# Mamba2 scan and gated feed-forward on one core: two pieces for weight blocks 8 to 11, a split join, and another order in the first scan

## The chip, the cores and the metric

The kernel runs on one core of a Trainium2 chip. The metric is the device time of one execution in microseconds (us); lower is better. Engines are TensorE (PE; its weight loads are listed as PEld), VectorE (DVE), ScalarE (ACT), GpSimd (POOL) and SyncE (SP), which here only issues transfers. SPq and DVEq stand for the sequencers of these engines. PSUM is the memory that PE writes its results to.

## The reference

```python
def _attn_ref(x, a, B, C):              # batch 4, 8 heads, 768 steps, 32 wide, state 16
    log_a = np.log(np.clip(a, 1e-06, 1.0))
    for c in range(nc):                 # chunks of 32 steps
        ...
        cum = np.cumsum(la, axis=-1)
        L = np.exp(cum[:, :, :, None] - cum[:, :, None, :]) * causal
        CB = np.einsum('bhin,bhjn->bhij', Cc, Bc)
        y_intra = np.einsum('bhij,bhjd->bhid', CB * L, xc)
        y_inter = np.einsum('bhin,bhnd->bhid', Cc, state) * decay_to_i[:, :, :, None]
        ...
        state = decay_full[:, :, None, None] * state + np.sum(Bx, axis=2)

def _moe_ref(x, w_in, w_out):           # 3072 tokens, 256 -> 2048 -> 256
    h = x @ w_in
    g = h * (1.0 / (1.0 + np.exp(-1.702 * h)))
    return (g @ w_out).astype(np.float32)
```

The scan's output (batch, step, head, width) is read as 3072 tokens of 256 values, the `x` of the second part. w_in and w_out come as float64.

## The kernel before, in words

**Groups.** The 3072 tokens are treated in six groups of 512 (`TG`). A group is made of two pairs, a pair being two chunks of 128 steps of one batch. For a group the kernel runs the scan of its two pairs, then the feed-forward. In the first group, `hidden(0, f)` makes `h` for one block of 128 hidden units after another, f = 0 to 15 (L878), each followed by the Silu on ACT, and `project_all(0, ...)` multiplies by w_out, again f = 0 to 15 (L976, tile `o`). Later groups use a form with seven products of sums of blocks (`X`, `Y`, `acc`), which needs all weights.

**Order.** Every engine executes its instructions in the order in which the program writes them (`in_order`). Where a piece of work stands in the text therefore decides what it can hold up. Work that goes with the first group's matmuls is put between blocks by `at(in_hidden[0], f, ...)`, which means after block f of `h`, and `at(in_project[0], f, ...)`, which means before block f of `o`.

**Weights.** The float64 weights are fetched as pairs of 32-bit words (`bits`) and made float32 on the chip. `PIECES` lists the pieces: of w_in blocks 0-1, 2-3, 4-5 and 6-7 (two blocks each), then 8-11 and 12-15 (four each); of w_out four pieces of four. `fetch(i)` issues two transfers on SP's queue. Then:

- `fields(i)`, VectorE, L193 and L196: exponent and mantissa bits out of the high words (tiles `p`, `m`);
- `clamp(i)`, ACT, L204 and L205: two steps on the exponent;
- `rounded(i)`, VectorE, L209: the low word is added to the mantissa;
- `join(i, parts)`, VectorE, L223 and L229: sign, exponent and mantissa become the weights, in one or several parts, two instructions for each part.

`narrow(i)` is the step of the schedule: it rounds piece i, joins it, and takes the fields of piece i + 1. For some pieces the join stands ahead of the next piece's fields, for others behind. In the kernel before the pieces that join first are 2, 4, 5 and 6; for piece 3 (blocks 6 and 7) the fields of piece 4 (blocks 8 to 11) come first. The pieces share four buffers, and a pair of two-block pieces shares one; `NEXT` says which piece is fetched after which join. Between piece 6 and its fields, `decay_rows(0)` runs for the next scan.

**First scan.** The first group's scan (pairs 0 and 1) is written out by hand at L1154 and below. Its steps: decays `L` from masked differences on PE and an exponential on ACT (L557); B and C transposed on VectorE (L597); `CT`, C masked by chunk part, for pair 0 (`mask_first(0)`) and pair 1 (`mask_first(1)`), both on POOL (L632); `pick_a`, copies of a picked by chunk part for the next group's decays (two ACT instructions, L364, tile `X`); `clip(az1)`, VectorE L354, which goes before it; `turn_back`, B back through PE (L609); `score`, the products of C and B (L664, tile `cb`, one area for both pairs); `since_first`, the running decay (`rows`, L515, and its exponential L520); `gain`, the chunks' states (L695, tile `A`, from x and `Be`); `weigh`, L times cb on VectorE (L675); `parts_first` and `since_start`, L649 on POOL, tile `CsT`; a scan over chunk states (L717) and `keep_first` with the states `S`; and in `finish`, `intra` (L818), `inter` (L804) and the copy of the result to `yT` (L838), with `fan_all` (L418) between the two pairs' `intra`. `dense(8, ...)` (L1150) is a product of ones into a PSUM bank that nobody reads. `fold_ident(1)` (L336) makes the second half of a constant that the next group's scan uses.

**x.** `load(p, "x")` issues two transfers of 128 KB for each pair, on SP.

Of the kernel before, what the change touches and what calls it, by code (L numbers as in the profile page):

```python
# [8 lines left out]
FP32 = mybir.dt.float32  # L9
# [26 lines left out]
def kernel(  # L36
# [101 lines left out]

    def load(p, parts=None):
        if parts is None:  # L140
            parts = "bcx" if p < 2 * PG else "bx"
            if p >= 2 * PG:
                load_blocks(p)
        for part in parts:
            dst, src, e = {"b": (rb, B, N), "c": (rc, C, N), "x": (rx, x, D)}[part]
            dst[p] = raw.tile([P, 2, NH, e], FP32, tag=part, name=f"{part}{p}",
                              bufs=2 if part == "c" else 3)
            for k in range(2):
                b, c = divmod(2 * p + k, NC)
                sl = slice(c * P, (c + 1) * P)  # L150
                nc.sync.dma_start(out=dst[p][:, k], in_=src[b, :, sl, :].rearrange("h s d -> s h d"))


    assert NF == 4 * CG
    PIECES = [("in", f, 2) for f in range(0, 8, 2)] + [("in", 8, 4), ("in", 12, 4)] \
        + [("out", f, 4) for f in range(0, NF, 4)]
# [56 lines left out]

    NEXT = {1: (6,), 5: (9,)}

    def join(i, parts=1):

        name, f, n = PIECES[i]
        n //= parts
        low, m, p2 = bits.pop(i)[1], mantissa.pop(i), power.pop(i)  # L220
        for k in range(parts):
            cols, fs = slice(k * n * DM, (k + 1) * n * DM), slice(f + k * n, f + (k + 1) * n)
            nc.vector.scalar_tensor_tensor(out=p2[:, cols], in0=low[:, cols], scalar=0x80000000,  # L223
                                           in1=p2[:, cols], op0=ALU.bitwise_and, op1=ALU.bitwise_or)
# [4 lines left out]
            nc.vector.scalar_tensor_tensor(  # L229
                out=dst, in0=m[:, cols].bitcast(FP32).rearrange("p (h e) -> p h e", h=h),  # L230
                scalar=2.0 ** -20, in1=p2[:, cols].bitcast(FP32).rearrange("p (h e) -> p h e", h=h),
                op0=ALU.mult, op1=ALU.mult)
        for n in NEXT.get(i, ()):
            fetch(n)

    def narrow(i):
        rounded(i)
        if i in (2, 4, 5, 6):
            join(i, 2 if i in (4, 5) else 1)
        if i == 6:  # L240
            decay_rows(0)
        if i + 1 < len(PIECES):
            fields(i + 1)
        if i not in (2, 4, 5, 6):
            join(i, 2 if i == 3 else 1)

# [37 lines left out]
    def table(f):  # L284

        nc.scalar.activation(early, early, f)
# [5 lines left out]
    load(0, "x")  # L292
    load(1, "x")

# [39 lines left out]
    def fold_ident(k, engine=nc.vector):  # L334
# [9 lines left out]
    nc.scalar.activation(cum, az0, AF.Ln)  # L344
    table(AF.Exp)
    nc.vector.tensor_tensor_scan(
        out=cum.rearrange("p k s -> p (k s)"), data0=carry.rearrange("p k s -> p (k s)"),
# [3 lines left out]

    def clip(t):

        nc.vector.tensor_scalar(out=t, in0=t, scalar1=1e-6, scalar2=1.0,  # L354
                                op0=ALU.max, op1=ALU.min)
        nc.vector.memset(t.rearrange(by_chunk, s=2)[:, :, :, 0], 0.0)

    def pick_a(p):

        assert divmod(2 * p, NC) == (0, CG)  # L360
        X = ffn.tile([P, 2, DM], FP32, tag="ob", name=f"X{p}")
        X = fans[p] = X.rearrange("p k (q i) -> p k q i", q=Q)
        for q in range(Q):
            nc.scalar.activation(X[:, :, q], az1, AF.Copy, scale=pick1[:, q:q + 1])  # L364

# [57 lines left out]
    def fan_all(p):  # L423

        ab = area(f"ab{p}")[:, :, :2 * Q * H]
        for r in range(R):
            fan(p, r, ab[:, r])
        fans[p] = ab

    def decay_fanned(p):  # L430
# [78 lines left out]
    def since_first():  # L509

        since[0] = ssd.tile([P, NC, P], FP32, tag="since", name="since0")
        rows = [bank(f"rows{p}")[:, :2 * P] for p in range(PG)]
        for p in range(PG):
            at = slice(32 * p, 32 * p + 32)
            nc.tensor.matmul(out=rows[p],  # L515
                             lhsT=whose[at, p].rearrange("p h n -> p (h n)"),
                             rhs=cum[at].rearrange("p k s -> p (k s)"), start=True, stop=True,
                             tile_position=(32 * p, 0), skip_group_check=True)
        for p in range(PG):
            nc.scalar.activation(since[0][:, 2 * p:2 * p + 2].rearrange("p c s -> p (c s)"),  # L520
                                 rows[p], AF.Exp)

    def drops():
# [102 lines left out]
    def mask_first(p):  # L626

        s = st[p]
        s["CT"] = ssd.tile([P, 2, Q, P], FP32, tag="CT", name=f"CT{p}")
        if p:  # L630
            nc.vector.memset(s["CT"][:, 0, 0, :1], 0.0)
        nc.gpsimd.tensor_tensor(  # L632
            out=s["CT"], in0=s["tp"].unsqueeze(2).to_broadcast([P, 2, Q, P]),
            in1=part.unsqueeze(1).unsqueeze(3).to_broadcast([P, 2, Q, P]), op=ALU.mult)
# [15 lines left out]

    def score(pairs, between=lambda: None, to=None):

        cb = (to or area(f"cb{pairs[0]}")).rearrange("p r (k e) -> p r k e", k=2 * PG)
        for n, p in enumerate(pairs):
            s = st[p]
            BT, CT = s["BT"], s.pop("CT")
            s["cb"] = cb[:, :, 2 * n:2 * n + 2]
            if n:
                between()
            for k in range(2):  # L660
                for i, side in enumerate(SIDES):
                    for r in range(R):
                        rows = slice(32 * r, 32 * r + 32)
                        nc.tensor.matmul(  # L664
                            out=s["cb"][side, r, k].rearrange("p (q i) -> p q i", q=Q),
                            lhsT=BT[rows, k, side], rhs=CT[rows, k, :, side],
                            start=True, stop=True, tile_position=(32 * r, H * i),
                            skip_group_check=True)
# [13 lines left out]

    def gain(pairs, to=None):
# [3 lines left out]
        for n, p in enumerate(pairs):  # L687
            Be = BE.pop(p)[0]
            for k in range(2):
# [80 lines left out]
    def finish(pairs, steps=range(2)):  # L770
# [39 lines left out]
        def intra(n, p):  # L810
            L = Ls[p]
            for k in range(2):
                for h in range(NH):
                    for i, side in enumerate(SIDES):
# [13 lines left out]
        if early:  # L828
            for n, p in enumerate(pairs):
                if n:  # L830
                    fan_all(PG)
                intra(n, p)
            for n, p in enumerate(pairs):
                for i in range(2):
                    inter(n, p, (i,))
            for t in range(NK):
                for i in range(2):
# [323 lines left out]
    turn_first("B")  # L1161
    clip(az1)
    differ_of(0)
# [5 lines left out]
    fields(0)  # L1169
    mask_first(1)  # L1170
    pick_a(PG)
# [41 lines left out]
    def store_a():  # L1213
# [14 lines left out]
    pairs = PG, PG + 1  # L1228
    at(in_project[0], 0, lambda: turn(PG), lambda: rounded(8),
       lambda: join(8), lambda: fields(9))  # L1230
    at(in_project[0], 1, lambda: clamp(9))
# [3 lines left out]
    at(in_project[0], 5, lambda: narrow(9))  # L1235
    at(in_project[0], 10, lambda: score(pairs), lambda: gain(pairs), lambda: keep_both(pairs, True),
# [203 lines left out]
```

## Time and profile before

| | before |
|---|---|
| runs, us | 346.44, 349.93, 346.78 |
| median, us | 346.78 |
| profiled execution, us | 347.67 |
| its span, first to last instruction, us | 345.9 |
| PE busy, share of the span | 98% |
| VectorE, ACT, POOL busy | 74%, 45%, 5% |
| granted clock | 1.00 |
| first `h` matmul of group 0, us from the start | 17.89 |
| first `o` matmul of group 0 | 47.23 |

Timeline rows read: start, length in us, engine, line, operation, tile written and tiles read, shape and count, and in brackets the idle time before it with what ended it. Rows of one line are put together where they follow each other, so a row's length with "x24" is that of 24 instructions. In the list of waits each line has the total in us, the number of waits and the longest. In the table of stretches each engine has its busy time and, in brackets, its instructions, followed by the granted clock, the mean share of the 16 DMA engines and the rate in GB/s.

### The profile page before, as it was taken

The page shows a single profiled execution, that of the slowest core. Times are in us where ns is not written, and L with a number is a line of the kernel's source. Part 1 is how long each engine was busy: PE and PEld are TensorE (multiplying, and loading weights), DVE is VectorE, ACT ScalarE, POOL GpSimd, SP SyncE. Part 2 cuts the span into 40 slices and gives each one's busy share as a digit, 9 for nine tenths or more (in the row PEclk, how much of TensorE's full clock was granted, in tenths as well). Part 3 has the DMA queues.
Part 4 walks back from the last instruction along what each step waited for, and adds up shares of the span by engine and source line. Part 5 has one row for each costly group of instructions (what it writes and reads, how often), then busy time and mean ns, then how long its engine had stood idle before and what let it go on. Part 6 is the DMA issues. An engine that isn't in the chain of part 4 may idle for free.

```text
span 345.9 us, 8116 instructions
## 1 busy us (share of the span) xinstructions
PE 339.2 (98%) x3380; PEld 270.2 (78%) x3380; DVE 256.1 (74%) x484; ACT 155.1 (45%) x352; POOL 16.7 (5%) x40
## 2 busy tenths in 40 slices
PE   8999999999999999999999999999999999999996
PEld 6633744555788888888888888888888888899996
DVE  5988999999799998858995667787564654465463
ACT  5786771507454324754332554442454322554320
POOL 7300110300000100000000000000000000000000
PEclk9999999999999999999999999999999999999999
DMA  6698899545637100435603036400000300000401
GB/s 160 132 289 211 217 239 133 152 67 102 122 63 127 36 0 15 65 99 100 110 27 51 2 78 121 64 0 3 0 4 2 62 2 0 0 2 0 63 0 62
DMA packets 90004, 25.76 MB, mean 74 GB/s; under 512 B 73416, under 2 KB 87248, under 8 KB 89968
## 3 DMA queue, kind: packets, MB, share of 16 engines
q1 hardware_dynamic: 89104, 24.72, 35.0%
q10 hardware_dynamic: 832, 0.52, 0.5%
q8 instruction: 26, 0.43, 0.5%
q14 instruction: 10, 0.08, 0.1%
q0 software_dynamic: 32, 0.01, 0.0%
HBM read 22.00 MB, written 3.24 MB: 73 GB/s over the span
## 4 chain that ended last, share of the span: by engine, by line
PE 92%; DMA 3%; SPq 2%; DVE 1%; issue 0%; ACT 0%; POOL 0%; DVEq 0%
PE acc L1039 28%; PE X L934 19%; PE Y L944 14%; PE o L976 8%; PE acc L1046 7%; PE h L878 7%; DMA bits<-in_moe_w_in_dram 3%; PE y L818 2%; PE cb L664 2%; SPq L181 1%; PE y L804 1%; PE A L695 1%; PE ab L536 1%; DMA az<-in_a_dram 1%; POOL CsT L649 0%
## 5 line engine op out<-in xcount | busy, mean ns | idle before, releaser
L939 ACT ACTIVATE ac<-X 128x256 f32<-128x256 f32 x76 | 29.1, 383 | 81.7 <-PE X L934 81.0
L1039 PE MATMUL acc<-mg,mw 128*128 128x256 f32 x192 | 54.5, 379 | 0.0
L1066 DVE TENSOR_TENSOR gT<-Y,ac 128x512 f32<-128x512 f32 x38 | 26.2, 689 | 38.1 <-PE Y L944 32.5
L911 ACT ACTIVATE gT<-gT 128x512 f32<-128x512 f32 (+1 forms) x76 | 38.9, 519 | 29.3 <-DVE gT L1066 28.8
L934 PE MATMUL X<-my,mi 128*128 128x256 f32 x152 | 45.2, 380 | 0.0
L1039 PEld LDWEIGHTS acc<-mg,mw 128*128 128x128 f32 x192 | 36.6, 190 | 4.9
L1066 DVE TENSOR_TENSOR gT<-Y,b 128x256 f32<-128x256 f32 x38 | 15.8, 419 | 28.5 <-PE Y L944 28.5
L878 PE MATMUL h<-yT,w_in 128*128 128x512 f32 (+1 forms) x92 | 35.5, 541 | 1.4 <-DVE w_in L229 0.9
L1039 PE MATMUL acc<-gT,w_out 128*128 128x256 f32 x128 | 35.5, 380 | 0.0
L878 PEld LDWEIGHTS h<-yT,w_in 128*128 128x128 f32 x92 | 17.2, 190 | 18.2 <-issue 12.8
L934 PEld LDWEIGHTS X<-my,mi 128*128 128x128 f32 x152 | 28.0, 190 | 4.0 <-ACT ac L939 0.3
L976 PE MATMUL o<-gT,w_out 128*128 128x512 f32 x64 | 28.3, 596 | 0.0
L902 DVE TENSOR_TENSOR mg<-gT 128x512 f32<-128x512 f32 x40 | 27.2, 681 | 0.0
L1039 PEld LDWEIGHTS acc<-gT,w_out 128*128 128x128 f32 x128 | 24.3, 190 | 3.4 <-ACT yT L853 0.2
L939 ACT ACTIVATE b<-X 128x256 f32<-128x256 f32 x38 | 14.6, 383 | 20.8 <-PE X L934 20.3
L934 PE MATMUL X<-yT,w_in 128*128 128x256 f32 x76 | 23.2, 389 | 0.0
L944 PE MATMUL Y<-yT,w_in 128*128 128x256 f32 x76 | 22.7, 381 | 0.0
L944 PE MATMUL Y<-my,mi 128*128 128x256 f32 x76 | 22.7, 381 | 0.0
L934 PE MATMUL X<-my,w_in 128*128 128x256 f32 x76 | 22.5, 380 | 0.0
L944 PE MATMUL Y<-yT,mi 128*128 128x256 f32 x76 | 22.5, 380 | 0.0
L976 PEld LDWEIGHTS o<-gT,w_out 128*128 128x128 f32 x64 | 11.9, 190 | 13.6 <-issue 12.7
L408 DVE TENSOR_TENSOR_SCAN L<-a,idents 128x1024 f32<-128x1024 f32 x9 | 20.5, 2279 | 0.3 <-DMA a<-scratch 0.3
(152 smaller groups left out, 547.8 us busy)
## 6 DMA issues: line engine op xcount, KB each, us to landing
a<-scratch SPq DMA_DIRECT2D x18, 256.0 KB, 4.9
bits<-in_moe_w_out_dram SPq DMA_DIRECT2D x8, 512.0 KB, 7.4
x<-in_x_dram SPq DMA_DIRECT2D x24, 128.0 KB, 3.7
out_dram<-ob SPq DMA_DIRECT2D x40, 64.0 KB, 2.0
bits<-in_moe_w_in_dram SPq DMA_DIRECT2D x8, 256.0 KB, 3.7
bits<-in_moe_w_in_dram SPq DMA_DIRECT2D x4, 512.0 KB, 11.4
b<-in_B_dram SPq DMA_DIRECT2D x20, 64.0 KB, 3.3
af<-in_a_dram SPq DMA_DIRECT2D x3, 384.0 KB
```

Of the source, the lines that this page charges most:

```text
L408: nc.vector.tensor_tensor_scan(out=L, data0=ra[p].rearrange("p k e -> p (k e)"), data1=idents.rearrange("p h i -> p (h i)"), initial=0.0, ...
L664: nc.tensor.matmul(out=s["cb"][side, r, k].rearrange("p (q i) -> p q i", q=Q), lhsT=BT[rows, k, side], rhs=CT[rows, k, :, side], start=Tru ...
L878: nc.tensor.matmul(out=h[:, cols], lhsT=w_in[:, f, k], rhs=yT[g][:, k, cols], start=(k == 0 and c == 0), stop=(k == NK - 1), skip_group_ch ...
L902: nc.vector.tensor_tensor(out=t[:, 0:2], in0=B[:, :, 1], in1=B[:, 0], op=ALU.subtract)
L911: nc.scalar.activation(o, i, AF.Silu, scale=GELU_SCALE)
L934: nc.tensor.matmul(out=s["X"], lhsT=lhsT, rhs=rhs, start=i == "1", stop=i == "4", skip_group_check=True)
L939: nc.scalar.activation(copy, s["X"], AF.Copy)
L944: nc.tensor.matmul(out=o, lhsT=lhsT, rhs=rhs, start=s.pop("new", False), stop=i != "5", skip_group_check=True)
L976: nc.tensor.matmul(out=o[c], lhsT=w_out[:, c, f], rhs=gT[g, f // 2][:, f % 2], start=(f == 0), stop=(f == NF - 1), skip_group_check=True)
L1039: nc.tensor.matmul(out=acc[g][0][i][:, cols], lhsT=w, rhs=h[:, cols], start=(j == 0 and k == 0 and (i, 0) in begins), stop=(j == NF // 2 - ...
L1046: nc.tensor.matmul(out=o[k] if type(o) is list else o[:, cols], lhsT=h[:, cols], rhs=w, start=(j == 0 and (i, k) in begins), stop=(j == NF ...
L1066: nc.vector.tensor_tensor(out=o, in0=v, in1=w, op=ALU.add)
```

## The change

1. x of pair 1: the first half is issued on SP as before, the second half from ACT's queue after the exponential's table is loaded.
2. w_in blocks 8 to 11 are two pieces of two blocks (pieces 4 and 5, sharing one buffer); later pieces' numbers go up by one. `fetch` and `NEXT` follow.
3. Piece 3 is joined in two parts: block 6 ahead of the fields of piece 4, block 7 behind them. Piece 1 (blocks 2 and 3) is joined in two parts; so are pieces 4, 5 and 6.
4. `fold_ident(1)` moves from the first scan's end to `narrow(7)`, ahead of that piece's join.
5. `clip(az1)` goes from VectorE to POOL; `pick_a` from two ACT instructions to one on POOL; `CT` of pair 1 from POOL to two ACT instructions (`mask_blocks`), without the memset ahead of it.
6. PE's order in the first scan: rows, scores of pair 0, states of pair 0, scores of pair 1, states of pair 1 (before: scores 0, rows, scores 1, states of both). In `intra` of the first scan the order is by heads.
7. `dense(8)` into a bank of its own becomes `dense(4)` into the free half of a bank of `rows`, and another `dense(4)` into a free part of `fan_all`'s area stands ahead of the first `h`.

```diff
-    def load(p, parts=None):
+    def load(p, parts=None, ks=range(2), queue=nc.sync):
...
-                nc.sync.dma_start(out=dst[p][:, k], in_=src[b, :, sl, :].rearrange("h s d -> s h d"))
+                queue.dma_start(out=dst[p][:, k], in_=src[b, :, sl, :].rearrange("h s d -> s h d"))
...
-    PIECES = [("in", f, 2) for f in range(0, 8, 2)] + [("in", 8, 4), ("in", 12, 4)] \
+    PIECES = [("in", f, 2) for f in range(0, 12, 2)] + [("in", 12, 4)] \
         + [("out", f, 4) for f in range(0, NF, 4)]
...
-    NEXT = {1: (6,), 5: (9,)}
-
-    def join(i, parts=1):
+    NEXT = {1: (7,), 5: (9,), 6: (10,)}
+
+    def join(i, parts=1, only=None):
...
     def narrow(i):
         rounded(i)
-        if i in (2, 4, 5, 6):
-            join(i, 2 if i in (4, 5) else 1)
-        if i == 6:
+        if i in (2, 4, 6, 7):
+            if i == 7:
+                fold_ident(1)
+            join(i, 2 if i in (4, 6) else 1)
+        if i == 7:
             decay_rows(0)
+        if i == 3:
+            join(i, 2, (0,))
         if i + 1 < len(PIECES):
             fields(i + 1)
-        if i not in (2, 4, 5, 6):
-            join(i, 2 if i == 3 else 1)
+        if i == 3:
+            join(i, 2, (1,))
+        elif i not in (2, 4, 6, 7):
+            join(i, 2 if i == 5 else 1)
...
-    load(1, "x")
+    load(1, "x", (0,))
...
     table(AF.Exp)
+    load(1, "x", (1,), nc.scalar)
...
-        for q in range(Q):
-            nc.scalar.activation(X[:, :, q], az1, AF.Copy, scale=pick1[:, q:q + 1])
+        nc.gpsimd.tensor_tensor(
+            out=X, in0=az1.unsqueeze(2).to_broadcast([P, 2, Q, P]),
+            in1=pick1.unsqueeze(1).unsqueeze(3).to_broadcast([P, 2, Q, P]), op=ALU.mult)
...
-            for k in range(2):
-                for h in range(NH):
+            for h, k in [(h, k) for h in range(NH) for k in range(2)] if early else [
+                    (h, k) for k in range(2) for h in range(NH)]:
...
+            dense(4, free)
             for t in range(NK):
...
-    clip(az1)
     differ_of(0)
...
-    mask_first(1)
+    mask_blocks(1)
+    clip(az1, nc.gpsimd)
     pick_a(PG)
...
-    score(range(PG), since_first, to)
+    free = since_first()
+    scores = score_steps(range(PG), to)
+    next(scores)
+    gain(range(PG), between=lambda: [None for _ in scores])
     weigh(0)
     weigh(1)
     drops()
-    gain(range(PG))
     parts_first()
     since_start(0, nc.gpsimd)
     fetch(1, held=nc.gpsimd)
-    for i in range(2, 6):
+    for i in range(2, 7):
         fetch(i)
...
-    dense(8, bank("dense"))
+    dense(4, free)
     finish(range(PG))
     join(0, 2)
-    fold_ident(1)
     fields(1)
     clamp(1)
     table(AF.Silu)
     rounded(1)
-    join(1)
+    join(1, 2)
...
-    at(in_hidden[0], 5, store_a, lambda: fetch(7), lambda: fetch(8),
-       lambda: load(PG + 1, "bc"))
+    at(in_hidden[0], 5, store_a, lambda: fetch(8))
+    at(in_hidden[0], 6, lambda: load(PG + 1, "bc"))
     at(in_hidden[0], 8, lambda: clip_rows(0))
-    for i, k, c in ((2, 1, 1), (3, 2, 2), (4, 4, 7), (5, 8, 10), (6, 10, 14), (7, 14, 15)):
+    for i, k, c in ((2, 1, 1), (3, 2, 2), (4, 3, 5), (5, 5, 7), (6, 8, 10), (7, 10, 14), (8, 14, 15)):
         at(in_hidden[0], k, lambda i=i: narrow(i))
         at(in_hidden[0], c, lambda i=i: clamp(i + 1))
```

More of the change, by code (lines that the diff above doesn't have):

```diff
@@ L145, in load @@
             dst, src, e = {"b": (rb, B, N), "c": (rc, C, N), "x": (rx, x, D)}[part]
-            dst[p] = raw.tile([P, 2, NH, e], FP32, tag=part, name=f"{part}{p}",
-                              bufs=2 if part == "c" else 3)
-            for k in range(2):
+            if 0 in ks:
+                dst[p] = raw.tile([P, 2, NH, e], FP32, tag=part, name=f"{part}{p}",
+                                  bufs=2 if part == "c" else 3)
+            for k in ks:
                 b, c = divmod(2 * p + k, NC)
                 sl = slice(c * P, (c + 1) * P)
-                nc.sync.dma_start(out=dst[p][:, k], in_=src[b, :, sl, :].rearrange("h s d -> s h d"))
+                queue.dma_start(out=dst[p][:, k], in_=src[b, :, sl, :].rearrange("h s d -> s h d"))
     assert NF == 4 * CG
-    PIECES = [("in", f, 2) for f in range(0, 8, 2)] + [("in", 8, 4), ("in", 12, 4)] \
+    PIECES = [("in", f, 2) for f in range(0, 12, 2)] + [("in", 12, 4)] \
         + [("out", f, 4) for f in range(0, NF, 4)]
@@ L211, in rounded @@
                                        op0=ALU.mult, op1=ALU.add)
-    NEXT = {1: (6,), 5: (9,)}
-    def join(i, parts=1):
+    NEXT = {1: (7,), 5: (9,), 6: (10,)}
+    def join(i, parts=1, only=None):
         name, f, n = PIECES[i]
         n //= parts
-        low, m, p2 = bits.pop(i)[1], mantissa.pop(i), power.pop(i)
-        for k in range(parts):
+        low, m, p2 = bits[i][1], mantissa[i], power[i]
+        for k in range(parts) if only is None else only:
             cols, fs = slice(k * n * DM, (k + 1) * n * DM), slice(f + k * n, f + (k + 1) * n)
@@ L232, in join @@
                 op0=ALU.mult, op1=ALU.mult)
-        for n in NEXT.get(i, ()):
-            fetch(n)
+        if only is None or parts - 1 in only:
+            for t in bits, mantissa, power:
+                t.pop(i)
+            for n in NEXT.get(i, ()):
+                fetch(n)
     def narrow(i):
         rounded(i)
-        if i in (2, 4, 5, 6):
-            join(i, 2 if i in (4, 5) else 1)
-        if i == 6:
+        if i in (2, 4, 6, 7):
[3 more added lines that the diff above has]
+        if i == 7:
             decay_rows(0)
+        if i == 3:
+            join(i, 2, (0,))
         if i + 1 < len(PIECES):
             fields(i + 1)
-        if i not in (2, 4, 5, 6):
-            join(i, 2 if i == 3 else 1)
+        if i == 3:
+            join(i, 2, (1,))
+        elif i not in (2, 4, 6, 7):
+            join(i, 2 if i == 5 else 1)
     scratch = dram.tile([NC, 2, NB * NH, H], FP32, name="scratch")
@@ L350, with clip @@
     fans, flat = {}, {}
[L352 to L356, printed above, removed]
+    def clip(t, engine=nc.vector):
+        engine.tensor_scalar(out=t, in0=t, scalar1=1e-6, scalar2=1.0,
+                             op0=ALU.max, op1=ALU.min)
+        engine.memset(t.rearrange(by_chunk, s=2)[:, :, :, 0], 0.0)
     def pick_a(p):
@@ L423, in fan_all @@
     def fan_all(p):
-        ab = area(f"ab{p}")[:, :, :2 * Q * H]
+        whole = area(f"ab{p}")
+        ab = whole[:, :, :2 * Q * H]
         for r in range(R):
@@ L428, in fan_all @@
         fans[p] = ab
+        return whole
     def decay_fanned(p):
@@ L511, in since_first @@
         since[0] = ssd.tile([P, NC, P], FP32, tag="since", name="since0")
-        rows = [bank(f"rows{p}")[:, :2 * P] for p in range(PG)]
+        whole = [bank(f"rows{p}") for p in range(PG)]
+        rows = [t[:, :2 * P] for t in whole]
         for p in range(PG):
@@ L521, in since_first @@
                                  rows[p], AF.Exp)
+        return whole[0][:, 2 * P:]
     def drops():
@@ L629, in mask_first @@
         s["CT"] = ssd.tile([P, 2, Q, P], FP32, tag="CT", name=f"CT{p}")
-        if p:
-            nc.vector.memset(s["CT"][:, 0, 0, :1], 0.0)
         nc.gpsimd.tensor_tensor(
@@ L649, in since_start, with score, score_steps @@
         engine.tensor_tensor(out=s["CsT"], in0=tp, in1=since[b][:, c:c + 2], op=ALU.mult)
-    def score(pairs, between=lambda: None, to=None):
+    def score(pairs, to=None):
+        for step in score_steps(pairs, to):
+            pass
+    def score_steps(pairs, to=None):
         cb = (to or area(f"cb{pairs[0]}")).rearrange("p r (k e) -> p r k e", k=2 * PG)
@@ L658, in score @@
             if n:
-                between()
+                yield
             for k in range(2):
@@ L681, in last_chunk, with gain @@
         return (4 * p + m + 1) % (2 * NC) == 0
-    def gain(pairs, to=None):
+    def gain(pairs, to=None, between=lambda: None):
         A = [(bank(f"A{pairs[0]}_{i}") if to is None else to[:, i, TG // 2:])[
@@ L687, in gain @@
         for n, p in enumerate(pairs):
+            if n:
+                between()
             Be = BE.pop(p)[0]
@@ L811, in intra @@
             L = Ls[p]
-            for k in range(2):
-                for h in range(NH):
+            for h, k in [(h, k) for h in range(NH) for k in range(2)] if early else [
+                    (h, k) for k in range(2) for h in range(NH)]:
                     for i, side in enumerate(SIDES):
@@ L830, in finish @@
                 if n:
-                    fan_all(PG)
+                    free = fan_all(PG)[:, 0, 2 * Q * H:]
                 intra(n, p)
@@ L1228 @@
     pairs = PG, PG + 1
-    at(in_project[0], 0, lambda: turn(PG), lambda: rounded(8),
-       lambda: join(8), lambda: fields(9))
-    at(in_project[0], 1, lambda: clamp(9))
+    at(in_project[0], 0, lambda: turn(PG), lambda: rounded(9),
+       lambda: join(9), lambda: fields(10))
+    at(in_project[0], 1, lambda: clamp(10))
     at(in_project[0], 2, lambda: clip_rows(1), lambda: decay(PG + 1),
@@ L1234 @@
     at(in_project[0], 4, lambda: turn(PG + 1))
-    at(in_project[0], 5, lambda: narrow(9))
+    at(in_project[0], 5, lambda: narrow(10))
     at(in_project[0], 10, lambda: score(pairs), lambda: gain(pairs), lambda: keep_both(pairs, True),
```

## The prediction

> **What bounds the kernel now.** I read the engine totals first, then the chain that ended last, TensorE's waits, and then the engines' timelines from 9 to 70 us. The totals and the chain's shares:
>
> ```profile
> PE 339.2 (98%) x3380; PEld 270.2 (78%) x3380; DVE 256.1 (74%) x484; ACT 155.1 (45%) x352; POOL 16.7 (5%) x40
> ...
> PE 92%; DMA 3%; SPq 2%; DVE 1%; issue 0%; ACT 0%; POOL 0%; DVEq 0%
> ```
>
> TensorE (PE) is busy nearly always. A change that leaves its work alone can win only what it waits for, and its list of waits is short; the three longest:
>
> ```profile
> PE busy L450 <- DVE ones L300: 1.2, 1, 1.2
> PE h L878 <- DVE w_in L229: 0.9, 1, 0.9
> PE h L878 <- ACT yT L838: 0.5, 1, 0.5
> ```
>
> The second line is the change's target. The chain (start, us, what) shows what it consists of:
>
> ```profile
> 17.15 9.61 DMA bits<-in_moe_w_in_dram
> ...
> 28.95 0.44 DVE w_in L229
> ...
> 29.52 17.43 PE h L878 x52
> ```
>
> w_in blocks 8 to 11 are on their way until 26.76. VectorE's `fields` (L193, L196) for them stands in the program ahead of the `join` (L223, L229) of block 6, which needs nothing from that transfer. So PE stops after block 5, at 28.50 by this table, and goes on at 29.52:
>
> ```profile
> 28.67:29.52 0.85, 0.00 (x0) 0.03 (x1) 0.82 (x3) 0.82 (x2) 0.00 (x0) 1.00 1.09 258
> 29.52:46.96 17.44, 17.44 (x54) 10.09 (x55) 16.61 (x25) 12.08 (x18) 2.20 (x3) 1.00 0.85 194
> 46.96:70.20 23.24, 23.24 (x176) 11.31 (x175) 22.75 (x30) 10.57 (x21) 3.08 (x4) 1.00 0.81 167
> ```
>
> The columns are stretch, length, then busy time of PE, PEld, VectorE (DVE), ScalarE (ACT) and POOL. PE has a hole of 0.85 us and none afterwards; but from 29.52 to 70.20 VectorE is busy 39.36 of 40.68 us. It is second in line right behind the hole.
>
> **The change part by part.** One block of `h` is four matmul records (blocks 10 to 12: eight of half the width). Reckoned as 64 of full width, they lie from 17.89 to 46.79, 28.90 us with two interruptions: 1.02 us (28.50 to 29.52, wait and refill) and 0.10 us at 21.43, where block 2 waited for the undivided join of blocks 2 and 3. Without them it is 27.78 us, 0.434 a record, 1.74 a block.
>
> *Block 6 ahead of `fields(4)`.* VectorE stood idle for 1.10 us before 27.28:
>
> ```profile
> 27.28 0.69 DVE L193 TENSOR_SCALAR p<-bits 128x1024 uint32<-128x1024 uint32 x1 [1.10 <-DMA bits<-in_moe_w_in_dram]
> ...
> 28.49 0.42 DVE L223 SCALAR_TENSOR_TENSOR p<-bits,p 128x256 uint32<-128x256 uint32 x1
> ...
> 29.29 0.42 DVE L223 SCALAR_TENSOR_TENSOR p<-bits,p 128x256 uint32<-128x256 uint32 x1
> ```
>
> One block's join takes 0.80 us (28.49 to 29.29). It waits for ACT's two clamps, 0.72 us each, behind the `fields` that ended near 25.4: ready near 26.8, joined by 27.7. PE wants block 6 at 28.4: the wait goes. `fields(4)`, now 512 columns, takes 0.75 (24.70 to 25.49 less refill) and block 7 another 0.80: ready near 29.3 against a need at 30.1. So 1.02 comes back here.
>
> *Join of blocks 2 and 3 in two parts.* Two 512-column records take 1.34 us (23.36 to 24.70), four of 256 columns 1.60 (28.49 to 30.09). The 0.26 more lies in VectorE's idle times of 0.41 and 0.48 at 20.06 and 23.36; block 2 comes earlier, and 0.10 comes back. Together PE could be 1.1 us ahead.
>
> *Blocks 8 to 11 as two pieces.* As one, VectorE spends 1.21 on fields, 1.13 on rounding and 2.66 on the joins: 5.0 us (27.28 to 28.49, 30.09 to 33.88). As two: 2 x (0.75 + 0.65 + 1.60) = 6.0. So +1.0 us of VectorE in the full stretch. SP issues two more transfers of 256 KB instead of large ones, about 0.5 us each in its queue, in front of az, af and w_out; those are wanted 10 us later.
>
> *`fold_ident(1)`* (0.60 us, 17.50 to 18.10) moves from a stretch with slack to the first w_out piece, just ahead of its join: +0.6, less the 0.53 us for which VectorE waited there for ACT (42.76).
>
> *What that does later.* VectorE's last join for w_out (blocks 12 to 15), against the matmuls that need it:
>
> ```profile
> 66.79 8.85 PE L976 MATMUL o<-gT,w_out 128*128 128x512 f32 x20
> ```
> ```profile
> 68.22 1.22 DVE L229 SCALAR_TENSOR_TENSOR w_out<-m,p 128x1024 f32<-128x1024 f32 x1
> ```
>
> PE reaches block 12 eight records into this group, which begins with block 10, at 70.2 to 70.3; the join ends at 69.4: 0.8 to 0.9 us of slack. In the new order VectorE fills its 1.10 us idle time, does 1.0 us more for blocks 8 to 11 and 0.6 for `fold_ident`, and saves 0.53: -1.10 + 1.0 + 0.6 - 0.53 = 0.0. Its last join still ends at 69.4, where PE, 1.1 us ahead, would want it at 69.1. PE waits and goes on near 69.5: **0.7 us** of the 1.1 is left. Behind it `inter` (75.57) has S since 71.2 and `intra` (76.54) the weighed L since 73.5, more than 3 us each, and from 92 us on VectorE waits for PE. So 0.7 lasts to the end.
>
> *First scan.* The second pair's CT goes from POOL (7.82 and 9.99, 1.04 each, behind a VectorE memset) to two ACT records in the place of the fan's picks (L364, 9.38 to 10.31). It is there 0.7 us earlier. PE's new order is rows 0.62, scores of pair 0 0.62, states A of pair 0 0.43, scores of pair 1 from about 11.05, against 11.08 now. What follows is set by weigh:
>
> ```profile
> 11.08 0.70 PE L664 MATMUL cb<-CT,Bt 32*64 32x128 f32 x32 [0.43 <-POOL CT L632]
> 11.71 0.86 PE L695 MATMUL A<-x,Be 64*32 64x64 f32 x64
> ```
> ```profile
> 11.88 2.35 DVE L675 TENSOR_TENSOR L<-L,cb 128x1024 f32<-128x1024 f32 x2 [0.31 <-PE cb L664]
> ```
>
> Weigh starts when the second pair's scores end, and the scan (14.15), S, yT and the first `h` (17.89) hang on it. So PE's 0.43 us is filled, by A, but the stage ends when it did: 0.0. The picks and `clip(az1)` on POOL (estimated from POOL's 1.04 for 512 columns as 0.6 + 1.1) end near 10.7; the fan uses them at 14.41. Dense matmuls: the 1.05 us before y (12.50 to 13.55) become 0.5 there, and 0.5 before `h`, under the 0.51 us that PE waits for yT anyway. Unknown are two things. PE's stop at 15.03 with no releaser (0.30, 0.5 with refill) may go once y starts earlier: 0 to -0.4 on the first `h`. And x of pair 1, second half, is issued from ACT near 6.4 instead of from SP at 8.36, ahead of the landing of pair 0's x (9.66 and 10.5). Its 128 KB at 170 GB/s are 0.75 us of all 16 DMA engines, so pair 0's x lands 0 to 0.75 later, and A now stands in front of the scores: 0 to +0.75 on the first `h`. I take 0 for each, as they pull opposite ways. At the end either shows less: as long as VectorE holds block 12 to 69.5, an earlier `h` wins nothing, and a later one costs only what goes beyond 1.1 - 0.7 = 0.4, so 0 to +0.35 for x.
>
> The Trainium skill, page "DMA: Bandwidth & Descriptors", section "Issuing engines are not separate DMA queues", says that transfers issued by several engines run on the same 16 DMA engines and interleave, so that another issuer saves issue time alone; by that the early x costs pair 0's x its share, and the sum would be up to 0.35 worse, 346.4.
>
> **Sum.** The profiled execution took 347.67 us: span 345.9 and 1.77 around it, 0.89 above the median of 346.78 of the three runs. Span 345.9 - 0.7 = 345.2, plus 1.77 is 347.0; at the median level, 346.78 - 0.7 = **346.1 us**.
>
> **Rivals.**
> *The whole gain (0.20).* PE's stop at 15.03 goes, h and VectorE's queue (clamp(1) stands behind yT on ACT) start 0.4 earlier, and the halved pieces cost VectorE less than 1.0: -1.1 to -1.5, 345.3 to 345.7. For it: half the idle times of VectorE at 18 to 24 us are waits for ACT. Against: between 42.8 and 69.4 VectorE has no idle time to give.
> *No gain (0.18).* If VectorE's queue is 0.8 later than now at block 12, the gain is gone: 346.8, give or take 0.2. For it: 1.6 us of added work against 1.63 of idle time, all of which must be usable. Pieces that land no earlier than now come to the same.
> *Slower, VectorE late at block 12 (0.15).* Each piece is handed to ACT for the clamps and back; where VectorE comes to the join too early it has waited 0.41, 0.48 and 0.53 us (20.06, 23.36, 42.76). With one piece more there is one such wait more, and if `fold_ident` does not fall into the 0.53, that stays too: -1.10 + 1.0 + 0.6 + 0.5 = +1.0, and with the waits of both half pieces +1.5. The join then ends at 70.4 to 70.9. From 70.3 on PE is later than now, by up to 0.6: 346.9 to 347.4. For it: from 29.5 to 70.2 VectorE has 1.3 us without work in all, of which the records' refill is a part. Against: `narrow` puts the rounding, and the join of the piece before, between a piece's fields and its join, which is there to cover the clamps.
> *Slower, PE at half rate (0.09).* PE's first records, eight of 128x192, took 2.93 us, 0.37 each, where `h`'s rate gives 0.16 (192/512 of 0.434). The clock column says 1.00 there too, so it doesn't rule out such a state. Half of the full-width work before y is taken away, and packed records of 32 or 64 rows fill the time. If PE fell back for 3.4 us (the cold stretch, 1.2 to 4.7), `h` would lose 1.7: 346.1 + 1.7 = 347.8. Against: PE is busy 10.84 of 12.23 us from 5.66 to 17.89, and will be so.
> The Trainium skill, page "TensorE: Matmul & The Clock Gate", section "Part 1: The HAM clock gate", has such a rule: half clock by default, let up after a busy window of some 3.4 us, and back after an idle one. It speaks for this rival, if packed work counts as idle.
>
> **The numbers.** Forecast 0.38 (345.8 to 346.5). The likeliest is 346.1; the range runs from the whole gain to the clock rival, 345.0 to 347.9. One per cent, 3.5 us, is about what a measurement of this kernel can tell from no change (one of the three runs is 3.2 above the others); no gain above reaches that, and a loss only if `h` fell back twice and kept no gain (350.2): faster 0.02, same 0.93, slower 0.05.
>
> **What would show it.** Right: no wait of `h` for w_in at 28.5; VectorE runs block 6's join before the fields of block 8; first `h` at 17.9, at most 0.4 off; a new PE wait for w_out of 0.2 to 0.6 us near 69. Wrong: first `h` after 18.3; waits for w_in at block 10 or 12 instead; no wait at 69; h's matmuls above 0.43 us.

## The result: 2.4 us slower

The changed kernel's median is 349.26 us (15 runs, 348.46 to 351.51) against 346.84 for the kernel before (15 runs, 346.34 to 349.93): ratio 1.0077, 95% interval 1.0060 to 1.0094, slower by 0.6 to 0.9%. The forecast was 346.1 in a range of 345.0 to 347.9; the loss lies outside it and on the other side.

The profiled execution of the changed kernel took 351.3 us with a span of 349.3. It is one of the longer ones of the fifteen, so a second trace was taken (349.13 us, span 347.1), and one more of the kernel before (346.85, span 345.1). TensorE's totals and the shares of the chain, from the page of the changed kernel:

```profile
PE 342.4 (98%) x3382; PEld 271.9 (78%) x3382; DVE 256.5 (73%) x490; ACT 155.2 (44%) x354; POOL 18.2 (5%) x42
...
PE 75%; DVE 15%; issue 3%; DMA 3%; ACT 2%; SPq 1%; POOL 0%; DVEq 0%; POOLq 0%
```

VectorE now has 15% of the chain that ends last (1% before): between 26 and 69 us the chain runs mostly over its instructions, not TensorE's. In the second trace VectorE has 2% of the chain, so this share is that of one execution; the wait of `A` for VectorE below is in both. The list of TensorE's waits, the four longest:

```profile
PE A L715 <- DVE m L210: 1.5, 1, 1.5
PE busy L464 <- DVE ones L310: 1.2, 1, 1.2
PE A L715 <- DVE CsT L663: 0.8, 1, 0.8
PE X L955 <- ACT ac L960: 0.3, 1, 0.3
```

The wait of `h` for w_in is gone, as forecast. Two others are there, both at a states product `A`: one in the first scan, one at 69.30 behind VectorE's `CsT`. TensorE's rows of the first scan and the table of stretches, in which the column after POOL is the granted clock:

```profile
10.00 0.69 PE L682 MATMUL cb<-CT,Bt 32*64 32x128 f32 x32
12.16 0.90 PE L715 MATMUL A<-x,Be 64*32 64x64 f32 x32 [1.47 <-DVE m L210]
12.99 1.16 PE L682 MATMUL cb<-CT,Bt 32*64 32x128 f32 x32
...
21.03 28.03 PE L899 MATMUL h<-yT,w_in 128*128 128x512 f32 x76
```
```profile
5.16:11.99 6.83, 5.28 (x158) 3.52 (x155) 5.20 (x10) 5.79 (x12) 6.25 (x11) 1.00 0.91 179
11.99:18.81 6.82, 6.65 (x212) 4.35 (x214) 4.54 (x8) 3.25 (x6) 1.61 (x4) 0.50 0.63 186
18.81:21.03 2.22, 2.22 (x108) 1.78 (x90) 2.08 (x6) 0.71 (x3) 0.00 (x0) 1.00 0.81 217
```

`A` of pair 0 stops TensorE for 1.47 us. The table of waits names VectorE's `m`, which doesn't feed `A`; a transfer lands in 16 parts, called stripes here, and the last stripe of the first half of pair 0's x landed at 12.03 in this trace (9.66 before), just ahead of `A`, so x is taken to be what ended the wait. Behind it stand the scores of pair 1 and weigh. The clock then is 0.50 for 6.82 us; the same 32 records of `cb` take 1.16 instead of 0.69. The first `h` comes at 21.03 instead of 17.89. From there to the end the two executions are alike, 349.3 - 21.03 = 328.3 against 345.9 - 17.89 = 328.0: the one has the hole of 0.85 us, the other the waits of 0.8 and 0.3 us at the second `A` and at `X`.

A part of the loss is not in the span at all. The time of an execution less its span has a median of 1.97 to 2.06 us in the changed kernel (here and in run 2) and in its versions of runs 3, 6, 13 and 14, and of 1.71 to 1.76 in the kernel before and in all versions of that. So some 0.25 us lie before the first or behind the last instruction; what they are is open.

### The profile page after: what moved, and what is told of

It reads as the page before. It is cut to its first block, busy times and chain, and to the rows that moved or that the text cites. A ratio compares the mean times of both kernels' runs of the same rounds, so it can differ in the third digit from the quotient of the medians.

```text
span 349.3 us, 8139 instructions
## 1 busy us (share of the span) xinstructions
PE 342.4 (98%) x3382; PEld 271.9 (78%) x3382; DVE 256.5 (73%) x490; ACT 155.2 (44%) x354; POOL 18.2 (5%) x42
## 4 chain that ended last, share of the span: by engine, by line
PE 75%; DVE 15%; issue 3%; DMA 3%; ACT 2%; SPq 1%; POOL 0%; DVEq 0%; POOLq 0%
PE acc L1060 25%; PE X L955 17%; PE Y L965 13%; PE acc L1067 7%; PE o L997 3%; DVE p L224 2%; PE y L838 2%; PE h L899 2%; PE cb L682 2%; DVE m L210 2%; PE A L715 2%; DMA a<-scratch 2%; PE y L824 1%; DVE p L194 1%; DVE m L197 1%
```

## The experiments

Each version was timed in turn with the kernel before, on the same chip. The kernel before has a median of 346.88 to 347.15 beside them, and each ratio is against these neighbours. Three theories stood at the start, by the letters of the expectations: X, pair 0's x lands late and holds up the first scan; C, the lower clock alone; W, VectorE is late by the split pieces. H, V, E, Q, P and I came with later runs and are stated there. The expectations number the runs otherwise: their second, third and fourth run are runs 3, 4 and 7 here, and "the last run" in run 14 is run 13.

**1. The kernel before, a second trace.** No edit.

> The kernel before, unchanged, for a second trace: the first one has a span of 345.9 us, the runs beside the other kernels have spans around 345.0. Theory H (the hole was an exception): in this trace w_in blocks 8 to 11 land about 1 us earlier than 26.76, the wait of h ahead of block 6 is under 0.3 us, and PE is on its way at the o of w_out earlier than 46.96. Rival: the hole of 0.85 us is there in a typical execution too, and the 0.9 us lie elsewhere.

Measured: 346.89 us; span 345.1. The hole is not there:

```profile
26.55 0.70 DVE L193 TENSOR_SCALAR p<-bits 128x1024 uint32<-128x1024 uint32 x1 [0.36 <-issue]
...
28.55 0.42 DVE L223 SCALAR_TENSOR_TENSOR p<-bits,p 128x256 uint32<-128x256 uint32 x1
```
```profile
17.83 28.39 PE L878 MATMUL h<-yT,w_in 128*128 128x512 f32 x76 [0.51 <-ACT yT L838]
...
65.33 0.79 PE L695 MATMUL A<-x,Be 64*32 64x64 f32 x56
```

Blocks 8 to 11 landed at 26.04 instead of 26.76, VectorE began their fields at 26.55 instead of 27.28, and TensorE waited 0.10 us for block 6, not 0.85. The 16 blocks of `h` take 28.22 us (17.83 to 46.05), 0.44 over the undisturbed 27.78; in this execution that is all there was to win there. The other 0.7 us belong to the first execution, whose time was 0.9 above the median. The hole comes back in the trace of run 11, again in an execution above its median.

**2. The changed kernel, a second trace.** No edit.

> The changed kernel again, for a second trace and its time beside the others. Theory X (x of pair 0 lands late): TensorE's wait at the states A of pair 0 appears again, 0.5 to 1.5 us, its end set by x. Theory C (clock alone): a stretch at clock 0.5 in every execution, and without one the time is that of the kernel before. Theory W (weights: VectorE later by the split pieces): first h near 17.9, and the loss arises after 46 us. Time by all three about 2.4 us above the kernel before.

Measured: 350.62 us, ratio 1.0104 (1.0081 to 1.0126). In this trace the clock is 1.00 throughout and the wait at `A` names its cause:

```profile
10.88 0.71 PE L715 MATMUL A<-x,Be 64*32 64x64 f32 x16
11.97 0.35 PE L715 MATMUL A<-x,Be 64*32 64x64 f32 x16 [0.38 <-DMA x<-in_x_dram]
12.25 0.69 PE L682 MATMUL cb<-CT,Bt 32*64 32x128 f32 x32
```

The last of the second half's 16 stripes landed at 11.93; the first `h` came at 18.75. The half clock is not in every execution (mean clock 0.990 or 0.995 in 2 of 15 and 2 of 6), and without it the kernel is still slower. So the clock alone (C) is out; both X and W have their wait. Executions near 351 us occur at full clock too (351.51 and 351.04 among the fifteen, 351.05 here); none of these was traced, so what they lose is open.

**3. Changed kernel, x on SP.**

```diff
-    load(1, "x", (0,))
+    load(1, "x")
...
-    load(1, "x", (1,), nc.scalar)
```

> The changed kernel with both halves of x of pair 1 issued from SP, as in the kernel before. Theory X: x of pair 0 has landed by 10.6 us, A starts behind the scores of pair 0 at once, the first h comes at 17.5 to 17.9, and the time falls by 2 to 3 us, to 346.0 to 347.0. Theory C: the half clock comes back in some executions even though A does not wait, time 348 or more. Theory W: no change from the changed kernel.

Measured: 348.86 us, ratio 1.0051 (1.0032 to 1.0070), no execution at a lower clock. The early x makes 0.3 to 0.5 points of the loss of 0.8 to 1.0 per cent (1.0077 and 1.0104 against 1.0051; beside run 2 the intervals are apart). The rest of the expectation was wrong: `A` waits still.

```profile
PE A L714 <- DMA x<-in_x_dram: 0.7, 1, 0.7
```

15 of the 16 stripes of pair 0's second half landed by 10.75, the last at 12.04. Such a late last stripe is there with the first scan of the kernel before too (10.65 and 11.57 in run 7), though not always (10.49 and 10.51 in the first trace of the kernel before); there `A` comes after the scores, and weigh doesn't wait for it.

**4. Kernel before, x early from ScalarE.** The edit of run 3 the other way round, on the kernel before.

> The kernel before with one thing alone: the second half of x of pair 1 is issued from ScalarE's queue. There A stands behind both scores (from 11.7 us), so weigh does not hang on x. Theory X: x of pair 0 lands at 10.6 to 12, at most 0.4 us of wait at A, and the time is within 0.3 us of the kernel before. Theory W: no change at all. If the early transfer harms by itself (clock or engines), the time is 1 us or more longer.

Measured: 351.20 us, ratio 1.0115 (1.0085 to 1.0144): the third case, harm by itself. TensorE's rows and the clock:

```profile
13.44 0.69 PE L697 MATMUL A<-x,Be 64*32 64x64 f32 x44 [0.91 <-issue]
...
18.65 1.06 PE L820 MATMUL y<-L,x 64*32 64x64 f32 x63 [1.83 <-issue]
```
```profile
18.81:25.64 6.83, 6.36 (x124) 3.94 (x112) 3.77 (x8) 4.21 (x9) 0.00 (x0) 0.50 1.07 347
```

Two stops without a releaser (`issue`: nothing that the profile shows ended them), and behind the second 6.83 us at half clock; four of the six executions have a mean clock of 0.989 or 0.995. The trace is of the longest of the six (352.37), and not all of its lateness is x's: the input `a` landed at 4.49 (3.89 in the first trace before), and TensorE's `ab` began at 6.57 instead of 5.66, while x was only issued at 6.43. On what the stops are, see run 14.

**5. Kernel before, x from ScalarE, later.**

```diff
     decay_exp(0, None, both[:, :, :2 * Q * H])
+    load(1, "x", (1,), nc.scalar)
```

> The kernel before with the second half of x of pair 1 on ScalarE's queue, but issued behind the first exponential, near 8.2 us, when SP issues it in the kernel before (8.36). Theory E (the early start is the harm: its packets take the engines from x of pair 0 and from the first half): time back near the kernel before, 346.9 to 347.5, clock 1.0 throughout. Rival Q (a second queue is the harm, whenever it starts): 349 to 351 as in the third run, with executions at a lower clock.

Measured: 347.05 us, ratio 1.0010 (1.0000 to 1.0020). So Q is out: the second queue costs 0.2% at most. Behind the first exponential in ScalarE's program the transfer does no harm that shows, ahead of it it costs 4 us by the medians. It didn't start near 8.2 as expected, but at 7.08, 0.65 us later than in run 4 (6.43) and, other than there, behind SP's issue of the first half (6.86).

**6. Changed kernel, x on SP, states behind both scores.**

```diff
-    scores = score_steps(range(PG), to)
-    next(scores)
-    gain(range(PG), between=lambda: [None for _ in scores])
+    score(range(PG), to)
     weigh(0)
     weigh(1)
     drops()
+    gain(range(PG))
```

> The changed kernel with x on SP (as in the second run) and with the states of both pairs behind both scores, as in the kernel before; the rest of the change stays. Theory X (the new place of the states lets the last x stripe hold up the scores and weigh): first h about 1.0 us earlier than in the run with x on SP alone, 17.8 to 18.0, time 347.6 to 348.0. Rival (the rest of the first scan is what is late): first h stays at 18.6 to 18.9, time 348.9.

Measured: 348.35 us, ratio 1.0028 (1.0013 to 1.0043), against 1.0051 for run 3: about 0.8 us by the middle values, though the intervals overlap. The trace is of the longest execution of twelve. In it `A` waits 0.52 us for x, now behind both scores, TensorE stops 0.71 us without a releaser ahead of the second `y`, and the first `h` comes at 18.72, so the early `h` that was expected is not shown.

**7. The weights' part alone, on the kernel before** (items 2, 3 and 4 of the change).

> The kernel before with the weights' part alone: blocks 8 to 11 as two pieces, split joins, fold_ident later. By the recorded sum: no wait of h at 28.5, 0.7 us faster than before (346.1). Theory W: VectorE is late for w_out blocks 12 to 15 or for the next scan, and it is 0.5 to 1.5 us slower. Theory X: not slower than before.

Measured: 348.07 us, ratio 1.0035 (1.0022 to 1.0049): slower, theory W. `h` runs 17.83 to 45.56 (the start of the next product) without a wait, 27.73 us, as the sum said. Then:

```profile
64.84 0.30 PE L704 MATMUL A<-x,Be 64*32 64x64 f32 x2
65.96 0.78 PE L704 MATMUL A<-x,Be 64*32 64x64 f32 x54 [0.83 <-DVE CsT L658]
```
```profile
65.48 0.42 DVE L658 TENSOR_TENSOR CsT<-tp,since 128x256 f32<-128x256 f32 x1
```

and of the kernel before, second trace:

```profile
64.72 0.42 DVE L649 TENSOR_TENSOR CsT<-tp,since 128x256 f32<-128x256 f32 x1
```

and of the kernel before, first trace:

```profile
65.50 0.42 DVE L649 TENSOR_TENSOR CsT<-tp,since 128x256 f32<-128x256 f32 x1
```
```profile
66.07 0.79 PE L695 MATMUL A<-x,Be 64*32 64x64 f32 x56
```

VectorE's `CsT` ends 0.76 later than in the second trace before. It is the last to read the PSUM bank `tp` of that pair, and by the code the second bank of `A` comes next in that ring of four. TensorE is there 0.5 us earlier, waits, and goes on 0.6 later (65.96 against 65.33). Another 0.35 is lost at 117.28, where `X` waits for ScalarE; that wait is in the five traces in which `A` waited about 0.8 us for `CsT` (changed kernel, runs 2, 6, 7 and 8), and in no other. Run 3, where `A` waited 0.43, doesn't have it.

**8. As 7, `fold_ident(1)` early again.**

> The weights' part alone, as in the fourth run, with fold_ident(1) back where the kernel before has it. Theory V: VectorE has 0.6 us less to do between 27 and 66 us, A waits 0.6 us less for the copy of C times decay (0.83 in the fourth run), and the time falls from 348.07 to about 347.5. Rival: fold_ident falls into idle time of VectorE in either place, and the time stays within 0.2 us.

Measured: 348.30 us, ratio 1.0023 (1.0003 to 1.0043). The time doesn't fall; `CsT` ends at 66.23, 0.3 later than in run 7. The join of blocks 2 and 3 already begins 0.3 later (20.02 against 19.72), and what VectorE has less to do later, 0.6, goes into the 0.54 us near 43 in which it waits for ScalarE and which are idle again. The late `fold_ident` is free, as the prediction had it.

**9. As 7, blocks joined whole.**

```diff
-    join(1, 2)
+    join(1)
...
-            join(i, 2 if i in (4, 6) else 1)
+            join(i, 2 if i == 6 else 1)
...
-            join(i, 2 if i == 5 else 1)
+            join(i)
```

> The weights' part as in the fourth run, but blocks 2 and 3, 8 and 9, 10 and 11 joined whole, two instructions for each instead of four: 6 instructions fewer, 0.8 us less on VectorE. Theory V: A waits up to 0.8 us less for the copy of C times decay (0.83 in the fourth run), time about 347.2 to 347.4. Rival (waits of h for a block that is joined later): new waits of h for w_in and 347.8 or more.

Measured: 346.62 us, ratio 0.9995 (0.9987 to 1.0004). Six short VectorE instructions fewer take 1.45 us from the median of run 7. `CsT` ends 0.70 earlier, at the time of the kernel before:

```profile
64.78 0.42 DVE L658 TENSOR_TENSOR CsT<-tp,since 128x256 f32<-128x256 f32 x1
```
```profile
64.88 1.16 PE L704 MATMUL A<-x,Be 64*32 64x64 f32 x56
```

The waits of `A` for `CsT` and of `X` are gone from the list, and no new wait of `h` came. The intervals of runs 7 and 9 are apart. Splitting the joins is what made the weights' part slower; the two pieces and block 6 first are not.

**10. Kernel before, block 6 first.** `join(3, 2, (0,))` ahead of the fields, `(1,)` behind; pieces as before.

> The kernel before with one thing alone: block 6 is joined ahead of the fields of blocks 8 to 11, block 7 behind them; the pieces stay as they were. If the hole is there in typical executions: 0.5 to 1.0 us faster than before. Theory H: within 0.3 us of before, either way. Theory V (VectorE's queue, at the copy of C times decay that frees a bank for the states A, takes back what PE wins): no gain either, and a wait of A for that copy at about 65 us.

Measured: 347.66 us, ratio 1.0016 (0.9996 to 1.0035): no gain, but not for the reason of theory V.

```profile
PE h L885 <- ACT gT L889: 0.7, 1, 0.7
```

ScalarE's clamp of blocks 8 to 11 stands ahead of the Silu of block 3 and waits for fields that now come behind a join; `h` waits for the bank that this Silu frees.

**11. Kernel before, `fold_ident(1)` late.**

> The kernel before with fold_ident(1) alone moved ahead of the first w_out join. Theory V (VectorE and PE arrive together at 65 us): VectorE fills its idle 0.54 us near 42 with it, its copy of C times decay ends near 64.6 instead of 65.15, w_in blocks 2 and 3 are there 0.6 us earlier, and PE, freed of 0.1 to 0.4 us, sets the end: 346.5 to 346.8. Rival: nothing moves, 346.9.

Measured: 346.80 us, ratio 0.9994 (0.9981 to 1.0008): not told apart from nothing. Its trace, of an execution of 347.32, has the hole of the first trace again:

```profile
29.12 17.43 PE L880 MATMUL h<-yT,w_in 128*128 128x512 f32 x52 [0.68 <-DVE w_in L229]
```

**12. Block 6 first, `fold_ident` late, clamp behind the Silu of block 3.**

> The kernel before with three things: block 6 joined ahead of the fields of blocks 8 to 11, fold_ident(1) late, and ScalarE's clamp of blocks 8 to 11 put behind the Silu of block 3 instead of block 2. Theory V: PE runs the 16 blocks of h without a wait (27.8 us), the wait for ScalarE's gT of the run with block 6 alone (0.67) is gone, VectorE's copy of C times decay ends near 64.7, A does not wait, and the time is 346.3 to 346.6, 0.3 to 0.6 below before. Rival: ScalarE or VectorE is late elsewhere, 346.9 or more.

Measured: 346.86 us, ratio 0.9994 (0.9978 to 1.0010). The mechanism came out (`h` 17.83 to 45.69 without a wait, none for `gT`, none of `A`; span 344.9), the gain didn't show: it is smaller than these intervals can tell.

**13. Changed kernel without the three causes** (x on SP, states behind the scores, joins whole).

> The changed kernel with the three suspected causes undone together: x of pair 1 on SP, the states behind both scores, blocks joined whole. What stays of the change: two pieces for blocks 8 to 11, block 6 ahead, fold_ident late, CT on ScalarE, picks and clip on POOL, rows first, the halved and moved dense products. If the three causes are all there is: as the run with whole joins, within 0.3 us of the kernel before (346.6 to 347.2), no wait of A for the copy of C times decay, clock 1.0. Rival (the rest of the first scan costs too, or the halved dense products let the clock fall): 347.6 or more, or executions with a mean clock under 0.998. A gain of the rest: 346.3 or less.

Measured: 347.63 us, ratio 1.0014 (0.9998 to 1.0031), no mean clock under 0.999. The ratio's distance from 1 is a fifth of the changed kernel's, but the time is 0.4 us above what was expected. Of the 0.66 us between the medians some 0.3 lie outside the span (2.06 against 1.72 us around it). The halved and moved dense products don't make the clock fall in any of these twelve executions; run 14, which has them too, has one of twelve at 0.995, and so has the kernel before in one of the 35 executions beside runs 1, 6, 8 and 10.

**14. As 13, POOL's picks behind the release of SP.**

```diff
     clip(az1, nc.gpsimd)
-    pick_a(PG)
...
     fetch(1, held=nc.gpsimd)
+    pick_a(PG)
```

> The kernel of the last run (three causes out, 347.63 against 346.97 before) with the picks on POOL moved behind the start of the w_in transfers. In the last run POOL's picks took until 11.88, its copy of C times decay and the word that releases SP came at 12.5 (12.1 in the kernel before), and VectorE waited 0.98 us for w_in blocks 2 and 3. Theory P (this late release is what is left of the loss): POOL is free at 10.2, SP starts at about 11.9, VectorE's wait at 18.2 is gone, and the time is 346.3 to 346.9. Rival I (PE's stop of 0.75 us ahead of the second y, which no engine explains, is what is left): the stop stays, first h at 18.1, time 347.4 to 347.8.

Measured: 348.01 us, ratio 1.0032 (1.0014 to 1.0049). SP's w_in transfers did start at 11.97 instead of 12.6, and the time didn't fall; whether it rose is open, as the interval overlaps that of run 13. Theory P falls. The trace is of one of the three longest executions (349.41), and TensorE's stops in it are longer than in run 13 (0.75 and 0.30):

```profile
16.25 1.01 PE L837 MATMUL y<-L,x 64*32 64x64 f32 x64 [0.98 <-issue]
...
22.68 1.55 PE L898 MATMUL h<-yT,w_in 128*128 128x512 f32 x3 [1.95 <-issue]
```

The DMA view of 20.1 to 21.2 us of this trace holds, among 246 packets of data, one of another kind:

```profile
q1 hardware_dynamic: 246, 0.24, 78.6%
q8 instruction: 1, 0.02, 5.0%
```

It is a packet of 16 KB on a queue for instructions, taken here as TensorE's, whose stops go with it. It lay from 20.19 to 21.07, and TensorE, stopped since 20.73, went on at 22.68. The earlier one, 13.69 to 14.85, precedes the go at 16.25. The stops of the other traces end in the same way, 1.3 to 1.6 us after such a packet: run 4, 12.11 then 13.44, and 17.16 then 18.65; run 13, 14.19 then 15.66; kernel before, first trace, 14.15 then 15.56. Where TensorE comes to the second `y` later, it doesn't stop: in the two traces of the changed kernel the packets ended at 15.11 and 14.31, and TensorE came there 3.2 and 1.9 us after them, at 18.31 and 16.17. The reading is that TensorE waits for its code, and that the code's packet comes late where it falls among w_in's or x's. No run changed this alone, so it is a reading of coinciding times and not shown by an experiment.

## Why the prediction was wrong, point by point

Three steps failed: the gain taken off the median, VectorE's deadline, and the two terms of the first scan that were put at nothing, the early x and the new order on TensorE. The weights' part, forecast at -0.7, measured +1.2 us (run 7); the terms put at nothing measured 0.9 to 1.8 and 0.8. Of the prediction's own signs of being wrong, "first `h` after 18.3" came: 21.03 and 18.75.

- **The hole.** The step that failed here is "at the median level, 346.78 - 0.7". The execution read had a hole of 1.02 us and a span 0.8 above that of the second trace; the hole was mostly what made it so (run 1). The prediction noted that it lay 0.89 us above the median, and still took a gain measured inside that execution off the median. In the second trace 0.44 us were to be had. (Its "28.50 by this table" is 28.67 in the table.)
- **Block 6, blocks 2 and 3.** Right: `h` takes 27.73 us in run 7 (27.78 was forecast), without a wait.
- **VectorE's sum.** Right in itself: +0.0 against the execution that was read (`CsT` ends at 65.91 in run 7, 65.92 there). Against the usual one it is +0.76, since of the 1.10 us of idle time only 0.36 is usual. The rival "VectorE late at block 12" had the right engine, but another place and another cause: w_out was not waited for.
- **The deadline.** Wrong: the 0.8 us of slack were taken at the last w_out join. The first thing that is late is `CsT`, ended 65.92, for `A` at 66.07: a slack of 0.15. `A` doesn't read `CsT`; it waits only for the PSUM bank to come free. Both rows stood in the trace from which the prediction was made. The gain that was to be left, 0.7, was therefore never there. That the changed kernel has a wait near 69 us, as forecast, is chance: it is `A`'s wait for `CsT`, at 69.30 because the first `h` came 3.1 us late, and at 67.03 in the second trace.
- **x on ScalarE's queue.** The price, "0 to +0.75 on the first `h`" and taken as 0, was mis-sized: `A` waited 1.47 and 0.38 in the two traces, and alone on the kernel before it cost 4.3 us by the medians (run 4 against its neighbours, 351.20 - 346.88). Why it costs so much more there than in the changed kernel is open. The prediction saw `A` in front of the scores, but put x's delay at the time of one transfer of 128 KB; what counts is the last of 16 stripes, up to 1.8 us behind the fifteenth. The rule cited from the Trainium skill, page "DMA: Bandwidth & Descriptors", section "Issuing engines are not separate DMA queues", that transfers interleave whichever engine started them, agrees with run 5, where the other queue costs 0.2% at most (1.0010); the 0.35 us that the prediction worked out from it are not what the early start cost (1.0115 in run 4, on the same queue).
- **TensorE's order.** The step "the stage ends when it did: 0.0" failed too: with the states of pair 0 ahead of the scores of pair 1, a late x holds up the scores and weigh. By runs 3 and 6 this is 0.8 us, not clear of the noise.
- **The clock.** The rival was real (0.50 for 6.83 us in two traces), but not on its ground: it went with stops of 1.47 and 1.83 us, and the halved dense products are neither needed for it (run 4 has the whole ones, and four of six executions at a lower mean clock) nor enough (run 13). A stop of 1.95 us in run 14 left the clock at 1.00. The Trainium skill's page "TensorE: Matmul & The Clock Gate", section "Part 1: The HAM clock gate", has windows of some 3.4 us that run freely; 6.83 is two of these, and mean clocks of 0.990 and 0.995 are 7 and 3.5 us at half in some 347. By its rule the clock goes back after an idle window; here stops of half a window went with it. Whether packed products count as idle, as the prediction asked, no run separates.
- **POOL.** `clip` and picks were put at 0.6 + 1.1, to end near 10.7; they took 1.13 and 1.04 to 1.59, ended at 11.50 in the first trace, and the release of SP came at 12.57 (12.11 before). By run 14 an earlier release doesn't pay.
- **TensorE's stop in the first scan.** "0 to -0.4", for a `y` that starts earlier, was wrong. In the changed kernel's two traces the stop is gone, but TensorE comes there later, not earlier, and nothing is won. Where `A` doesn't hold TensorE up so long it is back and longer: 0.71 to 0.98 us in runs 6, 13 and 14, and 1.83 in run 4.
- **Around the span.** The sum kept the 1.77 us; the changed kernel has 2.0. That is 0.25 us of the loss for which the sum had no term.
- **The class.** "same 0.93" came out, as a change under one per cent, but by luck: the time moved the other way, and with 15 executions on each side 0.6 to 0.9% is well told from nothing.

The parts, by the middle of the ratios and not additive: split joins about 1.4 us (runs 7 and 9), states ahead of the scores 0.8 (3 and 6), early x 0.9 to 1.8 (changed kernel, 2 and 3), what stays 0.5, not clear of nothing (13), of which some 0.3 lie around the span. Open is how much of the rest is TensorE's code. No version here is clearly faster than the kernel before; the best are runs 9, 11 and 12, at 0.9995 and 0.9994 with intervals that hold 1.

## What to carry to other kernels

Before pricing a wait, look whether the profiled execution is a usual one: a wait that is part of an execution slower than the median can't be taken off the median. Where TensorE and VectorE arrive together, look for the first of VectorE's results that TensorE needs, releases of PSUM banks included, and count instructions there: two of 256 columns took 0.80 us where one of 512 took 0.67. Where a product moves ahead of others in a queue, price it by the last stripe of its input, not by the usual landing.

## What the runs showed of the hardware that was not expected

- The last of the 16 stripes of a 128 KB transfer of x came up to 1.8 us after the fifteenth (10.75 and 12.04 in run 3; 10.21 and 12.03 in the changed kernel).
- TensorE's stops without a releaser ended 1.3 to 1.6 us after a 16 KB packet on an instruction queue, and lasted up to 1.95 us where w_in's transfers ran at the same time.
- Stops of 1.47 and 1.83 us went with 6.83 us at half clock in two traces (from 11.99 to 18.81 and from 18.81 to 25.64); one of 1.95 us in run 14 did not.
- The time around the span is 1.97 to 2.06 us in the changed kernel and its versions, 1.71 to 1.76 in the kernel before and its versions (medians).
